# Three delays in the planner of a fused attention and state-space kernel: cold filler matmuls, TensorE results and ScalarE results

## The chip, the cores and the metric

The kernel runs on one core of a Trainium2 chip. The metric is the device time of one execution in microseconds (us); lower is better. Twelve runs of the kernel before the change gave a median of 744.47 us, between 743.07 and 746.74. One of them was recorded by the hardware profiler.

## The reference

Two independent blocks read two inputs of shape (1, 2048, 640), and their outputs are put side by side to (1, 2048, 1280), all in bf16.

```python
# A: state-space block (S5)
dt = exp(log_dt); Lam_bar = exp(dt * Lam); B_bar = ((Lam_bar - 1) / Lam)[:, None] * Bmat
Bu = einsum("bld,pd->blp", x, B_bar)
h_t = Lam_bar * h_(t-1) + Bu_t                     # over 2048 steps, 640 complex states
y = 2 * real(einsum("blp,dp->bld", h, Cmat)) + x * Dskip
# B: attention with 32 query heads of 20 columns and one shared key/value head
q = x @ wq; k = x @ wk; v = x @ wv
p = softmax(q k^T * 20 ** -0.5)                    # 32 heads x 2048 x 2048
o = (p v) @ wo
out = concatenate([y, o], axis=-1)
```

The softmax is most of the work: 32 x 2048 x 2048 exponentials. The kernel cuts them into 2048 tiles of 128 keys x 512 queries.

## The kernel before, in words

**The tiles.** For every tile a score matmul (`score`, recorded at L637 as `SC<-QT,KT`) writes 128x512 scores into a bank of PSUM. Most tiles are exponentiated on ScalarE: one `ACTIVATE` at L1218 takes two or three neighbouring banks at once (128x1024 or 128x1536) and writes bf16 into the tiles `PR`. The others, 495 of the 2048, are exponentiated on VectorE and GpSimd: the scores are scaled so that a rounding to an int16 is the bit pattern of the exponential, the first evacuation on VectorE (L652 `BIG<-SC` or `BIG<-MB`, 683 ns) makes one shifted copy, and three more copies with added constants (L652 `BIG<-BIG` on VectorE, L647 `BIG<-BIG,step` on GpSimd) make a better approximation as a weighted sum of four. The weights sit in the value tiles `VS`. A value matmul (L637 `MB<-PR,VP` or `MB<-BIG,VS`) then multiplies each exponentiated tile into one shared output bank, in groups of up to four that run side by side in four column groups of the array.

**The slots.** Six PSUM banks form two slots of three (`SC0`, `SC1`). ScalarE works on one while TensorE refills the other. A refill is one step of the plan, called a fill (`Build.fill`). In 456 of the fills the third bank of the slot is given to a VectorE tile ("own" tile), and ScalarE then takes two banks. The next fill of that slot waits for both readers, the `ACTIVATE` and the evacuation. Two more banks (`MB`) serve everything else: the projections, the state-space block, VectorE tiles outside the slots and the output bank.

**The order.** Nothing in the order of instructions is written by hand. Python code plays a schedule forward in time (`Schedule.run`): each step has an engine, a duration in ns and the steps that it depends on, and an engine that is free picks the ready step of best priority (`Schedule.pick`). The order so found is then emitted, engine by engine, with semaphore waits between engines (`Emitter`). So the delays in the schedule are not executed by the chip; they decide only which instruction stands before which in the five in-order queues. The chip waits for the semaphores, however long that takes. 24 schedules are made with small random shifts of the background work, and the one with the earliest planned end is emitted (`planned`).

**Delays.** When a step is seen by another engine, its planned end and a delay by the engine that produced it are added up:

```python
def seen(self, op, eng):
    if op.dma_key is not None:
        return op.end + self.OUT["dma"]
    if op.eng == eng:
        return op.end + self.OWN[eng] if eng in self.OWN else op.end
    return op.end + self.OUT[op.eng]
```

`OUT` is this table. `begin` also registers the moments at which the schedule looks again (`lag`), which have to contain the delays.

**Fillers.** At the start TensorE has little to do, and `warm_source` offers it matmuls of zeros (`MB<-PR`, 128x512) at the lowest priority, whenever the plan has it idle. Later, `keep_source` offers small groups of zeros (`MB<-KT,VZ`, 256 columns) when too little was issued in the last 3 us of the plan.

**The start and the end.** The first `ACTIVATE` of the softmax needs the transposed input, the keys and the first queries, whose weights come by DMA (`BIG<-in_B_wq_dram`). After the last one come the last value matmuls, the evacuation of the output bank (`pvsb`, L1585 and L1587), the division by the row sums, the last output projection (`WO`, `BT`) and five stores.

Of the kernel before, what the change touches and what calls it, by code (L numbers as in the profile page):

```python
# [42 lines left out]
class Schedule:  # L43
# [3 lines left out]


    ENGINES = ("pe", "act", "dve", "pool", "sp")
    OUT = {"pe": 200.0, "act": 130.0, "dve": 110.0, "pool": 150.0, "dma": 60.0}  # L50
    OWN = {"pe": 0.0, "act": 60.0, "dve": 115.0, "pool": 100.0}
    URGENT = 1.0

# [51 lines left out]
# [8 lines that stand above are left out]
    def done(self, ops):  # L113
        return all(o.end is not None and o.end + self.OUT.get(o.eng, 60.0) <= self.t for o in ops)

# [12 lines left out]
    def begin(self, op, eng):  # L128
        if op.hook is not None:
            op.hook(op)  # L130
        op.start = self.t
        if op.late:
            self.late_from = self.t + op.dur + self.PAUSE
        if eng == "pe":
            if op.mode != self.mode:
                op.dur += self.SWITCH
                self.mode = op.mode
            self.loads.append((self.t, op.load))
        if op.port:
            if eng == "pool" and self.port_last["dve"] is not None:  # L140
                op.after.append(self.port_last["dve"])
            self.port_free[eng] = self.t + op.dur + (self.LOCK if eng == "pool" else 0.0)
            self.port_last[eng] = op
            self.at(self.port_free[eng])
        if op.dma_key is not None:
            self.free[eng] = self.t + op.tail * len(op.fns)
            s = max(self.t + 1300.0, self.dma_free.get(eng, 0.0), self.pipe)
            self.dma_free[eng] = self.pipe = s + op.dur
            op.end = max(s + op.dur + 700.0, self.free[eng] + 1700.0) + op.land
        else:  # L150
            if op.table is not None and op.table != self.table:
                self.table = op.table
                op.dur += self.TABLE
            op.end = self.t + op.dur + op.tail
            self.free[eng] = self.t + op.dur - (self.EARLIER.get(eng, 0.0) if op.psum else 0.0)
        self.order.append(op)
        self.at(self.free[eng])
        for lag in (0.0, 60.0, 100.0, 110.0, 115.0, 130.0, 150.0, 200.0):
            self.at(op.end + lag)

    stay = staticmethod(lambda: True)
# [253 lines left out]
class Build:  # L415
# [284 lines left out]
    def warm_source(self):  # L700

        if self.pv_first or self.s.t > 40000.0:
            return None
        p = self
        if self.started:
            if self.s.recent(3000.0) > self.WARM:
                return None
            fns = self.four(self.pvbank, [p.VZ[:]] * 4, p.KT[:, 0:512], True, True)
            return Op("pe", fns, self.mmt(512), prio=3.5, mode="C", load=512.0, reads=["VZ", "KT0"], writes=[self.pvbank.key],
                      deps=[self.c_op["VZ"], self.kt_op[0]])  # L710
        return Op("pe", [self.mm(self.pvbank.ap, p.PR[:, 0, 0:128], p.PR[:, 0, :], True, True)], 260.0, prio=9,
                  load=512.0, deps=[self.zero_op], reads=["PR0"], writes=[self.pvbank.key], hook=self.warm_last)

    WARM = 4500.0
    V_AT, BOUND_AT = (-88, -87), -99

# [467 lines left out]
    def fill(self, op, i):  # L1184
# [21 lines left out]
        if first:  # L1206
            other = self.slot_last[1 - i][0]
            begin = self.s.t + self.mmt(512, 4) + 200
            if other.eng == "act":
                begin = max(begin, other.start + other.dur if other.start is not None else self.s.t + other.dur)  # L1210
            first[0].due = begin + 2 * (0.8333 * 1024 + 64) - self.REFILL
# [478 lines left out]
    def o_task(self, qb, k, bank, early=False):  # L1690
# [28 lines left out]
        for i in range(begin, upto):  # L1719
            if last:  # L1720
                yield lambda: all(n in self.norm_op for n in steps[i][0])
            prev = part(i, prev, i == begin)
# [581 lines left out]
```

## Time and profile before

The profiled execution took 743.07 us, and its span, from the first to the last instruction, is 741.2 us; 1.9 us lie around it. It was the fastest of the twelve runs, 1.4 us below their median.

| | before |
|---|---|
| median of 12 runs | 744.47 us (743.07 to 746.74) |
| profiled execution | 743.07 us, span 741.2 us |
| first `ACTIVATE` of the softmax begins | 22.1 us |
| last one ends | 732.2 us |
| softmax `ACTIVATE` instructions | 676: 475 of 1024 columns, 201 of 1536 |
| busy share: TensorE, VectorE, ScalarE, GpSimd | 96%, 90%, 97%, 57% |
| granted TensorE clock, mean of the span | 1.000 |

"Busy" of TensorE counts every matmul from its start to its modelled end, and matmuls overlap; 96% is not 96% of what it can do. "PEld" is the load of the stationary operand, and it is the instruction that waits when a matmul's data are late. Rows of a group give its number, its busy time and the mean of one, then the idle time ahead of its instructions and the engine that ended it. Rows of the timeline give start and length, both in us, then engine, line and operation.

### The profile page before, as it was taken

The page shows a single profiled execution, that of the slowest core. Times are in us where ns is not written, and L with a number is a line of the kernel's source. Part 1 is how long each engine was busy: PE and PEld are TensorE (multiplying, and loading weights), DVE is VectorE, ACT ScalarE, POOL GpSimd, SP SyncE. Part 2 cuts the span into 40 slices and gives each one's busy share as a digit, 9 for nine tenths or more (in the row PEclk, how much of TensorE's full clock was granted, in tenths as well). Part 3 has the DMA queues.
Part 4 walks back from the last instruction along what each step waited for, and adds up shares of the span by engine and source line. Part 5 has one row for each costly group of instructions (what it writes and reads, how often), then busy time and mean ns, then how long its engine had stood idle before and what let it go on. Part 6 is the DMA issues. An engine that isn't in the chain of part 4 may idle for free.

```text
span 741.2 us, 26646 instructions
## 1 busy us (share of the span) xinstructions
PE 708.2 (96%) x11322; PEld 256.5 (35%) x11323; DVE 664.6 (90%) x1367; ACT 722.6 (97%) x702; POOL 425.8 (57%) x448
## 2 busy tenths in 40 slices
PE   9999899998999999999999999989999999999997
PEld 3322222234443533333333333323333333332333
DVE  7888999989788798998899999998998998988995
ACT  5999999999999999999999999999999999999995
POOL 3866566420266558367476674567654845778460
PEclk9999999999999999999999999999999999999999
DMA  9414444364220100101100010110000010100001
GB/s 196 81 35 130 92 116 84 94 141 76 48 52 18 25 20 21 51 11 34 43 25 24 15 32 19 39 47 19 18 15 19 10 33 23 37 16 17 26 15 37
DMA packets 78089, 34.43 MB, mean 46 GB/s; under 512 B 58852, under 2 KB 77972, under 8 KB 77972
## 3 DMA queue, kind: packets, MB, share of 16 engines
q1 hardware_dynamic: 76352, 32.34, 18.4%
q8 instruction: 90, 1.47, 0.8%
q10 hardware_dynamic: 1620, 0.39, 0.3%
q14 instruction: 27, 0.22, 0.1%
HBM read 11.53 MB, written 9.75 MB: 29 GB/s over the span
## 4 chain that ended last, share of the span: by engine, by line
ACT 61%; PE 32%; DVE 5%; DMA 1%; issue 1%; ACTq 0%; DVEq 0%
ACT PR L1218 60%; PE MB L633 11%; PE SC L637 11%; PE MB L637 10%; DVE BIG L652 1%; DMA BIG<-in_B_wq_dram 1%; DVE prod L647 1%; DVE W L652 1%; DVE CT L647 1%; DVE CA L647 1%; PE SC L633 0%; DVE CT L651 0%; DVE CA L651 0%; DVE g L2046 0%; DVE pvsb L1580 0%
## 5 line engine op out<-in xcount | busy, mean ns | idle before, releaser
L1218 ACT ACTIVATE PR<-SC 128x1024 bf16<-128x1024 f32 (+1 forms) x676 | 708.4, 1260 | 2.3 <-PE SC L637 1.1
L647 POOL TENSOR_TENSOR BIG<-BIG,step 128x512 int32<-128x512 int32 x401 | 407.0, 1043 | 285.3 <-DVE BIG L652 162.6
L652 DVE TENSOR_SCALAR BIG<-SC 128x512 int16<-128x512 f32 x456 | 302.5, 683 | 38.8 <-PE SC L637 35.4
L637 PE MATMUL SC<-QT,KT 32*128 32x512 bf16 x2009 | 264.5, 384 | 24.1 <-ACT PR L1218 16.8
L637 PE MATMUL MB<-BIG,VS 128*32 128x512 bf16 x1980 | 247.0, 384 | 1.2 <-issue 0.6
L637 PE MATMUL MB<-PR,VP 128*32 128x512 bf16 x1553 | 216.0, 385 | 0.8 <-DVE pvsb L1580 0.6
L637 PEld LDWEIGHTS SC<-QT,KT 32*128 32x128 bf16 x2009 | 68.1, 91 | 258.5 <-ACT PR L1218 167.5
L652 DVE TENSOR_SCALAR BIG<-BIG 128x1024 int16<-128x1024 int16 (+1 forms) x356 | 128.8, 418 | 7.7 <-PE MB L637 6.4
L637 PEld LDWEIGHTS MB<-BIG,VS 128*32 128x32 bf16 x1980 | 62.8, 95 | 65.4 <-issue 43.0
L637 PEld LDWEIGHTS MB<-PR,VP 128*32 128x32 bf16 x1553 | 53.6, 94 | 54.1 <-issue 40.9
L633 PE MATMUL MB<-CT,W 128*32 128x320 bf16 (+2 forms) x1040 | 49.8, 301 | 0.2 <-DVE BIG L2006 0.2
L633 PE MATMUL MB<-xaT,BT 128*32 128x256 bf16 x800 | 34.5, 274 | 0.0
L633 PE MATMUL MB<-xaT,BA 128*32 128x256 bf16 x800 | 33.6, 274 | 0.1
L633 PE MATMUL MB<-CA,W 128*32 128x512 bf16 (+1 forms) x640 | 31.2, 302 | 0.0
L647 DVE TENSOR_TENSOR prod<-MB,tab 128x1024 bf16<-128x1024 f32 x20 | 24.3, 1215 | 3.8 <-PE MB L633 3.8
L652 DVE TENSOR_SCALAR BIG<-MB 128x512 int16<-128x512 f32 x39 | 26.5, 680 | 1.1 <-PE MB L637 0.7
L633 PEld LDWEIGHTS MB<-CT,W 128*32 128x32 bf16 x1040 | 21.5, 96 | 16.9 <-issue 7.9
L633 PE MATMUL MB<-WO,OP 128*32 128x128 bf16 (+1 forms) x576 | 26.5, 297 | 0.1
L1761 DVE CAST stg<-MB 128x512 bf16<-128x512 f32 x35 | 23.9, 682 | 2.6 <-PE MB L633 2.4
L633 PE MATMUL MB<-BIG 128*32 128x512 bf16 x340 | 25.6, 383 | 0.0
L2046 DVE TENSOR_TENSOR_SCAN g<-sc,hst,prod 128x256 bf16<-128x256 f32 x30 | 23.1, 774 | 0.0
L633 PEld LDWEIGHTS MB<-xaT,BA 128*32 128x32 bf16 x800 | 19.1, 96 | 9.0 <-issue 5.4
(167 smaller groups left out, 419.8 us busy)
## 6 DMA issues: line engine op xcount, KB each, us to landing
out_dram<-stg SPq DMA_DIRECT2D x31, 128.0 KB, 1.8
qd<-BIG SPq DMA_DIRECT2D x20, 128.0 KB, 1.8
QT<-qd SPq DMA_DIRECT2D x28, 80.0 KB
OP<-pvsb SPq DMA_DIRECT2D x105, 20.0 KB
rdP<-recs SPq DMA_DIRECT2D x105, 20.0 KB
W<-in_A_B_re_dram SPq DMA_DIRECT2D x10, 160.0 KB, 2.8
W<-in_A_B_im_dram SPq DMA_DIRECT2D x10, 160.0 KB, 2.8
lbd<-W SPq DMA_DIRECT2D x10, 160.0 KB, 1.9
```

Of the source, the lines that this page charges most:

```text
L633: r = e.matmul(out[32 * j:32 * j + 32], lhsT=lhsT[:, 32 * j:32 * j + 32], rhs=rhs, start=start, stop=stop, tile_position=(0, 32 * j), skip ...
L637: return lambda e: e.matmul(out, lhsT=lhsT, rhs=rhs, start=start, stop=stop, **kw)
L647: return lambda e: e.tensor_tensor(out, a, b, op)
L652: return lambda e: e.tensor_scalar(out, a, s1, s2, op0=op0, op1=op1)
L1218: ex = self.act(lambda e: e.activation(dst, t[:, 0:512 * n], ACT.Exp, scale=1.0 / UNIT), 0.8333 * 512 * n + 64, table="exp", deps=[op], re ...
L1761: ev = self.dve(lambda e: e.tensor_copy(st, bank.ap), 645, deps=[prev], reads=[bank.key], writes=[key], prio=self.EV, gate=(lambda: last.e ...
L2046: o = self.dve(lambda e, ri=ri, init=init: e.tensor_tensor_scan(p.g[:, u, ri, :], rdec, p.prod[:, 1, 0, ri, :], init, ALU.mult, ALU.add), ...
```

## The change

Three edits, all in the planner. The delay after which another engine sees a TensorE result in the plan goes from 200 to 215 ns, that of a ScalarE result from 130 to 225 ns; the list of moments at which the schedule looks again follows. A filler matmul at the start is planned at 450 ns until 6.0 us of planned time and at 240 ns after that, in place of 260 ns throughout.

```diff
-    OUT = {"pe": 200.0, "act": 130.0, "dve": 110.0, "pool": 150.0, "dma": 60.0}
+    OUT = {"pe": 215.0, "act": 225.0, "dve": 110.0, "pool": 150.0, "dma": 60.0}
...
-        for lag in (0.0, 60.0, 100.0, 110.0, 115.0, 130.0, 150.0, 200.0):
+        for lag in (0.0, 60.0, 100.0, 110.0, 115.0, 150.0, 215.0, 225.0):
...
-        return Op("pe", [self.mm(self.pvbank.ap, p.PR[:, 0, 0:128], p.PR[:, 0, :], True, True)], 260.0, prio=9,
+        return Op("pe", [self.mm(self.pvbank.ap, p.PR[:, 0, 0:128], p.PR[:, 0, :], True, True)], self.COLD if self.s.t < self.WARMED else 240.0, prio=9,
                   load=512.0, deps=[self.zero_op], reads=["PR0"], writes=[self.pvbank.key], hook=self.warm_last)
 
+    COLD, WARMED = 450.0, 6000.0
     WARM = 4500.0
```

No instruction is computed differently. What differs is the emitted order, and with it which tiles go to which engine. The counts of the two emitted programs:

| instructions | before | after |
|---|---|---|
| softmax `ACTIVATE`, 1024 columns | 475 | 463 |
| softmax `ACTIVATE`, 1536 columns | 201 | 210 |
| tiles exponentiated by ScalarE / by VectorE and GpSimd | 1553 / 495 | 1556 / 492 |
| first evacuations on VectorE from a slot (`BIG<-SC`) / from `MB` | 456 / 39 | 443 / 49 |
| copies of two tiles on VectorE / of one tile | 327 / 29 | 344 / 30 |
| copies of two tiles on GpSimd | 401 | 379 |
| fillers at the start (`MB<-PR`, 512 columns) | 23 | 16 |
| small zero matmuls (`MB<-KT,VZ`, 256 columns) | 356 | 292 |
| all instructions on TensorE (matmuls) | 11320 | 11244 |

The number of DMA issues is the same. The last `ACTIVATE` of the softmax has 1024 columns before and 1536 after.

## The prediction

> **What bounds the kernel now.** I read the page's busy shares first, then the costliest groups with shapes kept apart, then the waits, and last the timeline at the start, at one stall and at the end.
>
> ```profile
> PE 708.2 (96%) x11322; PEld 256.5 (35%) x11323; DVE 664.6 (90%) x1367; ACT 722.6 (97%) x702; POOL 425.8 (57%) x448
> ACT  5999999999999999999999999999999999999995
> ```
>
> ScalarE is full in 38 of 40 slices, so its length is the span.
>
> ```profile
> L1218 ACT ACTIVATE PR<-SC 128x1024 bf16<-128x1024 f32 x475 | 448.3, 1118 | 1.5 <-PE SC L637 1.0
> L1218 ACT ACTIVATE PR<-SC 128x1536 bf16<-128x1536 f32 x201 | 278.1, 1597 | 0.8 <-PE MB L637 0.4 <-PE SC L637 0.2
> ```
>
> Only 2.3 us of idle time are named in front of these, but a mean of 1118 ns hides stalls, because a record that waits or drains is long. Reading the 676 records one by one, from start to start, no 1024 is under 903 ns and no 1536 under 1330. The softmax runs from 22.14 to 732.17 us, 710.0 us. 474 intervals at 903, 201 at 1330 and the last record (about 1.2) make 696.5. **13.5 us are stall**, nearly all behind 1024s: 61 stalls over 50 ns hold 11.0 us, the rest are crumbs. With 22.1 ahead and 9.0 behind, these are all that the order can win without moving tiles off ScalarE.
>
> ```profile
> PEld SC L637 <- ACT PR L1218: 167.5, 414, 1.2
> POOL BIG L647 <- DVE BIG L652: 162.6, 41, 38.3
> PEld SC L637 <- DVE BIG L652: 60.7, 145, 0.9
> ```
>
> A fill stands at the head of TensorE's queue and waits 167.5 us in all for ScalarE to free the slot: the plan puts it there too early, and work that could run meanwhile stands behind it. One stall:
>
> ```profile
> 474.57 10.70 ACT L1218 ACTIVATE PR<-SC 128x1024 bf16<-128x1024 f32 x11
> ...
> 477.74 0.39 PE L637 MATMUL SC<-QT,KT 32*128 32x512 bf16 x3
> 478.06 0.39 PE L637 MATMUL MB<-BIG,VS 128*32 128x512 bf16 x2
> 478.34 0.83 PE L633 MATMUL MB<-CT,W 128*32 128x512 bf16 x12
> 479.10 0.39 PE L637 MATMUL SC<-QT,KT 32*128 32x512 bf16 x3
> ```
>
> The fill at 479.10 is issued behind 14 other matmuls; ScalarE starts on it 0.44 us later, at 479.54, 1300 ns after its last start where 903 would do. Sorting the 61 by what the fill last waited for: 12 (2.4 us) begin within 90 ns of the end of the slot's VectorE evacuation, 49 (8.6 us) stand behind other matmuls in TensorE's queue.
>
> **The change part by part.** The new delays run nowhere; they reorder. The delays of the trace: fill to `ACTIVATE` is 437 to 444 ns, which less the 219 ns that the plan gives a fill is 218 to 225, so 215 is right. From the planned end of an `ACTIVATE` (917 ns after its start) to the next fill of its slot it is never under 150 ns, and half of them are over 360, queues included. 130 was below anything seen; 225 lies above the floor.
>
> *Tiles.* ScalarE gets 12 fewer 1024s and 9 more 1536s: 9 x 1.330 - 12 x 0.903 = **+1.1 us**, on the path, with no cover; certain to some tenths.
>
> *Stalls behind TensorE's queue (8.6 us).* Between two fills the plan now leaves up to 95 ns more for other groups before the fill. I priced the emitted orders with trace rows (216 ns for a group of 512 columns, from nine fillers in 2.12 us with a last drain of 0.38; about 95 for a change between score and other groups, the fill issues 308 after such a group): gaps between fills whose TensorE work exceeds ScalarE's interval by over 100 ns are 139 before, 124 after; over 200 ns, 65 and 56. If stalls fall with that count, 11% of 8.6 is 0.9 us. If each of the 49 shrinks by the 95 ns by which the plan was short, it is 4.7. A smaller gain would need the new order to be worse where it counts better. The long stalls, such as the 397 ns above, come from three or more groups in a row, which 95 ns does not break; I take **-2.5**, between.
>
> *Stalls behind VectorE (2.4 us).* VectorE gets 17 more two-tile copies (429 ns each), one more single (286) and 3 fewer first evacuations (683): +5.5 us on an engine with 76.6 us idle, since GpSimd makes 22 fewer. GpSimd itself, 57% busy, is on no path. Against it, 13 fewer fills (443 for 456) have an evacuation of their own to wait for. The bound below is -0.5 (a fifth of these stalls gone); above, +3, if over half of the 5.5 lands in front of evacuations that a fill waits for. I take **+0.4**, nearer to the small end, because 60.7 us of such waits on TensorE cost ScalarE only 2.4 now.
>
> *Fillers.* In the trace a filler costs 427 ns cold and 216 warm, and the granted clock is full from 4.6 us on.
>
> ```profile
> 1.24 2.32 PE L637 MATMUL MB<-PR 128*128 128x512 bf16 x5 [1.24 <-DVE sel L755]
> ...
> 6.25 2.12 PE L637 MATMUL MB<-PR 128*128 128x512 bf16 x9
> 8.21 1.06 PE L637 MATMUL SC<-ident,CT 128*128 128x128 bf16 x16
> 9.42 0.39 PE L637 MATMUL MB<-BIG 128*20 128x512 bf16 x4 [0.16 <-DMA BIG<-in_B_wq_dram]
> ```
>
> The plan thought that 20 fillers of 260 would be through before the transposes of 8.21; they were late. Now 12 stand there, and the transposes can start up to 1.0 us earlier. But the next group waits for the query weights, which land at 9.29 whatever TensorE does, and from 9.42 to 18.26 TensorE never waits, with the same work after as before. So the first softmax `ACTIVATE` stays at 22.1: **0**, from -0.3 (transposed tiles ready earlier) to +0.3 (five more small value matmuls ahead of the first fill).
>
> What speaks against it is the clock. By the rows, after 4.6 us fillers cost 216, yet the plan charges 450 until its 6.0 us, which is 6.9 of the profile, as its zero is VectorE's first memset at 0.91. So TensorE will idle about 0.2 us per filler there, and some 0.7 ahead of the transposes and 1 ahead of the weights. [...] Bounding it from rows alone: if the 8.8 us of work from 9.42 ran cold for 3.4 us (the time from the first matmul at 1.24 to 4.63), it would lose 1.7 us. I keep that as a small risk.
>
> *The end.* Before, the last `ACTIVATE` has 1024 columns and only one or two value groups remain after it:
>
> ```profile
> 732.02 0.59 PE L637 MATMUL MB<-BIG,VS 128*32 128x512 bf16 x5
> 732.24 0.38 PE L637 MATMUL MB<-PR,VP 128*32 128x512 bf16 x2
> 732.45 0.82 PE L633 MATMUL SC<-WO,OP 128*32 128x512 bf16 x12
> ...
> 736.47 0.61 PE L633 MATMUL SC<-BT,pvsb 128*32 128x512 bf16 x8
> ```
>
> `pvsb` starts at 732.68, 0.5 us after ScalarE's last record ends. After, five groups of output projection and then 13 value matmuls (four groups, the first with the last tiles) follow that end in the queue: 24 value matmuls and 20 projections after the last fill (about 2.4 us) end some 0.2 us behind it, then 4 x 0.213 and a drain of 0.39, so `pvsb` starts 1.2 us after it: +0.7. Three projection groups that ran after the division (736.04 and around) now run before: -0.64 on TensorE, but the last of three VectorE outputs ends only 0.25 before ScalarE's store, so -0.25. Together **+0.5**, from 0 to +0.9.
>
> 64 small zero matmuls less (16 groups of 110 ns) are free: TensorE waits 167.5 us anyway. DMA issues on SP keep their number; their waits are not on the chain.
>
> Sum: 1.1 - 2.5 + 0.4 + 0 + 0.5 = **-0.5 us**: 742.6 against the profiled 743.07, and 744.0 against the median of 744.47, which lies 1.4 above it. About 0.2% (1.5 us) is what a measurement of this kernel can tell from no change.
>
> **The rivals.**
>
> *Order wins (faster).* ScalarE's stalls behind TensorE's queue shrink by the whole 4.7 and VectorE costs nothing: 1.1 - 4.7 + 0.5 = -3.1, 741.4. For: the 167.5 us of waits at fills, and that 130 lies below the least delay of the trace. Against: the long stalls come from bunched groups, and 124 of 139 stay.
>
> *VectorE holds the fills (slower).* The copies that GpSimd gave up stand in VectorE's queue ahead of evacuations of slots; each late evacuation holds the fill at L637 and all of TensorE behind it, and ScalarE stalls. Price: +3 in place of +0.4, with only 0.9 won behind TensorE: 1.1 - 0.9 + 3 + 0.5 = +3.7, 748.2. It decides once stalls behind VectorE exceed about 5 us (2.4 now). For: 90% busy and 5.5 us more. Against: 13 fewer such fills.
>
> *It does nothing (no change).* The chip waits by semaphore and not by plan; the change only draws another order of like quality: 1.1 + 0.5 = +1.6 with the stalls unchanged, 746.1, the upper edge of no change.
>
> **How the numbers follow.** The forecast (stalls down by 1 to 3.5, the sum within 1.5 of zero) gets 0.38; order wins, 0.31; VectorE holds, 0.20; no gain at all, 0.11, of which half falls in no change. So faster 0.32, same 0.40, slower 0.28, some of the forecast's edges going to either side. The range for 8 in 10 goes down to -3.6 (4.7 and a VectorE gain of 0.5) and up to +3.5, short of the slow rival's centre: 740.9 to 748.0.
>
> **What would show it.** Right: the softmax begins at 22.1 +-0.3; its records sum to 697.5 without stalls, and stalls are 11 to 12 us; waits of `PEld SC L637` for ScalarE fall below 167.5; `pvsb` starts over 1 us after the last softmax record. Wrong: stalls above 13.5 or below 9; over 5 us of them begin within 90 ns of an evacuation; a granted clock below full after 5 us; a first `ACTIVATE` beyond 22.6.

## The result, and the profile after

The changed kernel takes **751.49 us** (median of 8 runs, 749.67 to 753.39; a ninth, at 749.84, is on record with its clock), 0.9% more than before: ratio 1.0090, 95% interval 1.0074 to 1.0105. That is 7.5 us above the forecast and 3.5 above the upper end of the range. The profiled execution took 751.28 us with a span of 749.5, against 741.2 before.

The page first: busy shares, ScalarE's slices and the granted clock's slices.

```profile
PE 713.8 (95%) x11246; PEld 255.3 (34%) x11247; DVE 662.5 (88%) x1382; ACT 725.7 (97%) x699; POOL 401.6 (54%) x426
ACT  5799999999999999999999999999999999999995
PEclk9799999999999999999999999999999999999999
```

ScalarE's share is still 97%, but its second slice (18.7 to 37.5 us) has dropped from 9 to 7, and so has the clock there. Before, every slice of the clock was a 9. The shares say nothing of this: VectorE and TensorE are even a little less busy.

The groups of the softmax `ACTIVATE`, shapes kept apart (count, then busy time and mean in ns, then idle time before them):

```profile
L1219 ACT ACTIVATE PR<-SC 128x1024 bf16<-128x1024 f32 x463 | 439.3, 1101 | 6.7 <-PE SC L637 4.5 <-PE MB L637 1.4
L1219 ACT ACTIVATE PR<-SC 128x1536 bf16<-128x1536 f32 x210 | 290.8, 1633 | 0.5 <-PE SC L637 0.5
```

The counts are those of the emitted program. Idle time ahead of the 1024s has grown from 1.5 to 6.7 us. Read from start to start, with 903 and 1330 ns taken off as before, the span splits so:

| us | before | after | difference |
|---|---|---|---|
| first softmax `ACTIVATE` begins | 22.12 | 22.38 | +0.26 |
| records without stalls, last record included | 696.55 | 697.68 | +1.13 |
| stalls while the clock is full | 13.50 | 14.69 | +1.19 |
| stalls while the clock is at half | 0 | 5.06 | +5.06 |
| after the last softmax record | 9.06 | 9.74 | +0.68 |

The differences add up to 8.3, which is that of the two spans. Some 60% of it arises while TensorE runs at half clock: in the profiled run from 28.94 us for 10.24 us, and from 424.89 for 3.41. The windows around the first of them show it. Each row has the window, its length, then busy time (and instructions) of PE, PEld, VectorE, ScalarE and GpSimd, then the granted clock; the last two numbers are the share of the DMA engines and GB/s. Before:

```profile
25.53:28.94 3.41, 3.10 (x36) 1.13 (x28) 2.83 (x8) 3.41 (x5) 3.07 (x7) 1.00 0.44 98
28.94:32.36 3.42, 3.36 (x53) 1.37 (x51) 2.30 (x7) 3.42 (x5) 2.91 (x7) 1.00 0.19 43
32.36:35.77 3.41, 3.41 (x46) 0.97 (x46) 2.70 (x6) 3.41 (x4) 2.00 (x3) 1.00 0.11 38
35.77:39.18 3.41, 3.41 (x48) 0.86 (x40) 3.09 (x6) 3.41 (x5) 3.18 (x4) 1.00 0.13 43
```

After:

```profile
25.53:28.94 3.41, 2.95 (x41) 1.69 (x38) 3.31 (x15) 3.41 (x5) 3.03 (x7) 1.00 0.39 88
28.94:32.36 3.42, 3.42 (x32) 0.94 (x28) 1.49 (x4) 2.81 (x3) 2.94 (x8) 0.50 0.18 40
32.36:35.77 3.41, 3.41 (x24) 0.48 (x21) 1.68 (x3) 2.05 (x2) 0.69 (x2) 0.50 0.10 33
35.77:39.18 3.41, 3.41 (x28) 0.65 (x25) 1.98 (x3) 2.05 (x2) 2.04 (x2) 0.50 0.10 34
```

In the three windows at half clock TensorE is busy without a break and issues 84 matmuls (32, 24, 28) in place of 147 (53, 46, 48). ScalarE works 2.05 of 3.41 us in two of them and waits for fills. For these 10 us TensorE is the bound and not ScalarE. What came just before is in the timeline of TensorE (start, length, engine, line, operation, number). Before:

```profile
23.88 0.39 PE L637 MATMUL SC<-BIG 128*20 128x512 bf16 x4
24.20 0.39 PE L637 MATMUL SC<-QT,KT 32*128 32x512 bf16 x2
24.52 0.61 PE L637 MATMUL SC<-BIG 128*20 128x512 bf16 x8
25.06 0.39 PE L637 MATMUL SC<-QT,KT 32*128 32x512 bf16 x2
25.38 0.61 PE L637 MATMUL SC<-BIG 128*20 128x512 bf16 x8
...
27.18 0.40 PE L637 MATMUL MB<-PR,VP 128*32 128x512 bf16 x4
```

After:

```profile
22.57 1.04 PE L637 MATMUL SC<-BIG 128*20 128x512 bf16 x16
23.54 0.39 PE L637 MATMUL SC<-QT,KT 32*128 32x512 bf16 x2
23.86 0.39 PE L637 MATMUL SC<-BIG 128*20 128x512 bf16 x4
...
25.29 0.39 PE L637 MATMUL SC<-QT,KT 32*128 32x512 bf16 x2 [0.28 <-ACT PR L1219]
25.51 0.28 PE L986 MATMUL MB<-mab,pick 20*128 20x1 f32 x2
25.72 0.29 PE L936 MATMUL SC<-wvr,BIG 128*128 128x20 bf16 x5
...
27.12 0.39 PE L637 MATMUL SC<-QT,KT 32*128 32x512 bf16 x2 [0.31 <-ACT PR L1219]
27.35 0.28 PE L986 MATMUL MB<-mab,pick 20*128 20x1 f32 x2
...
28.36 0.61 PE L637 MATMUL MB<-PR,VP 128*32 128x512 bf16 x8
```

Between the fills stand matmuls of 1 and of 20 columns. They fill the "busy" column, because the profile gives each of them 0.16 to 0.27 us up to its modelled end, however few its columns. A better measure is to count each matmul by its columns at 0.417 ns, side-by-side ones once; then one of 20 columns counts for 8 ns. (The third group of 512 columns in a row follows the second at 427 ns at half clock, in after at 31.21 us, and at 216 at full clock, in before at 31.08; the count takes half of the 427, 0.417 a column.) This estimate gives the share of a window in which columns stream: **42%** in 25.53 to 28.94, and **39%** in 421.47 to 424.89, the two windows after which the clock falls. No gap between streams in them is longer than 0.6 us. In before, the same stretch from 25.53 to 28.94 has 60%; the thinnest windows of its profiled run have 45% and 48%, and the clock stays full. Before, the second query projection (`SC<-BIG`, 20 matmuls with 512 columns) was spread from 23.88 to 25.99 between fills, and the first value matmul came at 27.18. After, 16 of the 20 stand in one block from 22.57 to 23.6 ahead of the third fill, and the first value matmul comes at 28.36; from 24.4 to 28.4 only the fills themselves and one other group (at 26.09) are wide.

The waits (total, number, longest):

```profile
PEld SC L637 <- ACT PR L1219: 163.4, 400, 0.9
POOL BIG L647 <- DVE BIG L652: 161.5, 52, 22.8
...
PEld SC L637 <- DVE BIG L652: 56.9, 131, 0.9
```

Both waits of the fills have gone down, from 167.5 and 60.7, and yet the stalls have gone up, from 13.5 to 19.8 us. One reading is that the fills that wait less came later to the head of TensorE's queue.

The end is as predicted. The last softmax record ends at 739.80, and `pvsb` starts 1.16 us later:

```profile
738.18 1.62 ACT L1219 ACTIVATE PR<-SC 128x1536 bf16<-128x1536 f32 x1
...
740.96 0.38 ACT L1586 ACTIVATE pvsb<-MB 128x256 bf16<-128x256 f32 x1 [1.16 <-PE MB L637]
```

**All runs, not one.** Each run has a mean granted clock, and (1 - clock) x 2 x span is the time that it spent at half clock, as the clock records of the traces of before and after hold 1.0 and 0.5 alone (13.5 us by this for the profiled run of after, 13.65 in its trace). In 110 runs of before the median is 4.5 us, in 9 of after 13.5. Fitted over the runs, each us at half clock costs 0.28 us before and 0.39 after; at full clock the fits give 743.3 and 746.5. So of the 7 us between the medians about 3.8 belong to half clock (13.5 x 0.39 - 4.5 x 0.28 = 4.0; the slope of after, from nine runs, is uncertain by 0.07, which makes about 1 us here) and about 3.2 would remain at full clock. In the profiled runs that is tiles 1.1, stalls 1.2, end 0.7, start 0.26. No run of after was at full clock, so its 746.5 is an extrapolation.

### The profile page after: what moved, and what is told of

Its sections match the earlier page's. It is cut to its first block, busy times and chain, and to the rows that moved or that the text cites. A ratio compares the mean times of both kernels' runs of the same rounds, so it can differ in the third digit from the quotient of the medians.

```text
span 749.5 us, 26447 instructions
## 1 busy us (share of the span) xinstructions
PE 713.8 (95%) x11246; PEld 255.3 (34%) x11247; DVE 662.5 (88%) x1382; ACT 725.7 (97%) x699; POOL 401.6 (54%) x426
## 3 DMA queue, kind: packets, MB, share of 16 engines
q1 hardware_dynamic: 76352, 32.34, 18.7%
## 4 chain that ended last, share of the span: by engine, by line
ACT 63%; PE 31%; DVE 2%; SPq 1%; DMA 1%; issue 0%; DVEq 0%
ACT PR L1219 63%; PE SC L637 10%; PE MB L637 10%; PE MB L633 10%; DVE BIG L652 1%; PE SC L633 1%; SPq L622 1%; DMA BIG<-in_B_x_dram 1%; DVE prod L647 1%; PE SC L936 0%; SPq L618 0%; DVE PR L647 0%; DVE pvsb L1581 0%; DVEq L470 0%; DVE pvsb L1588 0%
## 5 line engine op out<-in xcount | busy, mean ns | idle before, releaser
L647 POOL TENSOR_TENSOR BIG<-BIG,step 128x512 int32<-128x512 int32 x379 | 382.8, 1039 | 316.2 <-DVE BIG L652 161.5
L652 DVE TENSOR_SCALAR BIG<-SC 128x512 int16<-128x512 f32 x443 | 294.2, 683 | 38.4 <-PE SC L637 35.9
L637 PE MATMUL SC<-QT,KT 32*128 32x512 bf16 x1999 | 265.5, 387 | 24.5 <-ACT PR L1219 17.7
L637 PE MATMUL MB<-PR,VP 128*32 128x512 bf16 x1556 | 218.3, 387 | 0.4 <-DVE pvsb L1581 0.4
L637 PEld LDWEIGHTS SC<-QT,KT 32*128 32x128 bf16 x1999 | 68.0, 91 | 261.0 <-ACT PR L1219 163.4
L652 DVE TENSOR_SCALAR BIG<-BIG 128x1024 int16<-128x1024 int16 (+1 forms) x374 | 135.4, 419 | 6.1 <-PE MB L637 4.3
L637 PEld LDWEIGHTS MB<-BIG,VS 128*32 128x32 bf16 x1968 | 60.4, 95 | 68.6 <-issue 45.7
L652 DVE TENSOR_SCALAR BIG<-MB 128x512 int16<-128x512 f32 x49 | 33.3, 680 | 4.7 <-PE MB L637 4.6
L633 PE MATMUL MB<-xaT,BT 128*32 128x256 bf16 x800 | 37.0, 275 | 0.0
L633 PE MATMUL MB<-WO,OP 128*32 128x128 bf16 (+1 forms) x576 | 27.5, 297 | 0.0
L633 PEld LDWEIGHTS MB<-CT,W 128*32 128x32 bf16 x1040 | 20.6, 96 | 17.8 <-issue 9.5
L1581 DVE CAST pvsb<-MB 128x512 bf16<-128x512 f32 x31 | 21.2, 682 | 5.5 <-PE MB L637 5.1
L633 PEld LDWEIGHTS MB<-xaT,BT 128*32 128x32 bf16 x800 | 19.4, 96 | 11.1 <-issue 8.8
```

What stands on the lines that cost most here:

```text
L633: r = e.matmul(out[32 * j:32 * j + 32], lhsT=lhsT[:, 32 * j:32 * j + 32], rhs=rhs, start=start, stop=stop, tile_position=(0, 32 * j), skip ...
L637: return lambda e: e.matmul(out, lhsT=lhsT, rhs=rhs, start=start, stop=stop, **kw)
L647: return lambda e: e.tensor_tensor(out, a, b, op)
L652: return lambda e: e.tensor_scalar(out, a, s1, s2, op0=op0, op1=op1)
L1581: ev = self.dve(lambda e: e.tensor_copy(p.pvsb[:, slot, :], bank.ap), 645, deps=[op], reads=[bank.key], writes=[f"pvsb{slot}", f"pvsb{slot ...
```

## The experiments

Three theories. A: the order has thin windows, the clock falls after them, and the stalls of those stretches are the loss. B: the longer delays themselves make a worse order at full clock. C: the fillers bring the clock up late, and all else follows from that. Against all stood the rival that the change only drew an unlucky order. The table has all runs; "falls" are those of the profiled run before the end of the softmax, and stalls are split by whether the clock was full or at half. The ratio is estimated from all runs and need not be the quotient of the two medians.

| kernel | median us | ratio to before, 95% interval | us at half clock, median | falls at, us | stalls at full / at half clock, us |
|---|---|---|---|---|---|
| after | 751.49 | 1.0090 (1.0074 to 1.0105) | 13.5 | 28.9, 424.9 | 14.7 / 5.1 |
| e_fill | 747.30 | 1.0026 (1.0003 to 1.0048) | 10.4 | none | 14.4 / 0 |
| e_delays | 748.59 | 1.0078 (1.0040 to 1.0115) | 10.5 | 99.1, 594.1 | 14.9 / 2.9 |
| e_early | 751.45 | 1.0087 (1.0060 to 1.0113) | 17.2 | 27.6, 505.5 | 13.7 / 5.8 |
| e_dense | 750.33 | 1.0085 (1.0056 to 1.0114) | 6.7 | 421.8 | 17.7 / 0.5 |
| e_dense2 | 750.67 | 1.0062 (1.0037 to 1.0088) | 11.2 | 28.8, 424.8, 506.7 | 14.7 / 4.9 |
| e_seed23 | 749.77 | 1.0068 (1.0048 to 1.0088) | 10.5 | 27.5, 423.4 | 14.7 / 3.1 |
| e_before5 | 744.85 | 1.0011 (0.9987 to 1.0036) | 0.7 | none | 14.3 / 0 |
| e_act150 | 750.54 | 1.0073 (1.0050 to 1.0097) | 12.0 | none | 12.6 / 0 |
| e_lateq | 747.68 | 1.0038 (1.0023 to 1.0052) | 6.7 | none | 17.8 / 0 |
| e_akeep | 748.43 | 1.0054 (1.0035 to 1.0073) | 14.9 | 27.2, 593.8 | 13.2 / 3.3 |
| e_bkeep | 747.82 | 1.0054 (1.0033 to 1.0075) | 6.0 | 25.4, 510.1 | 13.2 / 7.0 |
| e_bdense | 744.73 | 0.9997 (0.9987 to 1.0008) | 3.0 | 500.7 | 14.0 / 1.1 |
| e_fillq | 750.77 | 1.0083 (1.0059 to 1.0106) | 17.2 | 26.6, 504.5 | 14.4 / 5.8 |
| e_bq | 743.17 | 0.9981 (0.9962 to 1.0000) | 0.7 | 716.0 | 14.1 / 1.5 |
| e_act180q | 748.12 | 1.0042 (1.0026 to 1.0057) | 10.4 | 26.6 | 15.0 / 2.0 |
| e_150q | 745.95 | 1.0020 (0.9999 to 1.0041) | 0 | none | 13.4 / 0 |
| e_bthin | 747.95 | 1.0047 (1.0031 to 1.0062) | 23.1 | 167.3, 501.8 | 13.3 / 1.6 |
| e_bwide | 745.96 | 1.0022 (1.0011 to 1.0034) | 4.5 | 501.2 | 14.6 / 1.8 |

The kernel before had a median between 744.34 and 744.66 beside these runs.

### One part of the change at a time

The delays alone (e_delays), and the filler edit alone (e_fill):

```diff
 e_delays
-    OUT = {"pe": 200.0, "act": 130.0, "dve": 110.0, "pool": 150.0, "dma": 60.0}
+    OUT = {"pe": 215.0, "act": 225.0, "dve": 110.0, "pool": 150.0, "dma": 60.0}
 e_fill
-        ... 260.0, prio=9,
+        ... self.COLD if self.s.t < self.WARMED else 240.0, prio=9,
```

> The two delays alone (215 and 225 ns), the filler planned at 260 ns as before. The query projection stands spread between the fills here, as in before. Theory A: no fall at 29 us, so the clock term is gone; what is left is the tiles (1 fewer 1024 than before, so -0.9 us), the end (last instruction of 1536 columns, up to +0.7) and the other stalls: 743 to 747. Theory D (the delays make the slower order): 748 or more without any fall.

> The filler's edit alone (450 ns until 6.0 us, then 240), delays 200 and 130. The query projection stands bunched in front of the third fill as in after, but the first value matmul comes two fills earlier. Theory A: a fall near 29 us if the window there holds under about 43% of matmul time: 747 to 750; without a fall, 744 to 746 (the tiles are those of before). Theory D: as before, 744.6.

Each alone is slower than before, by 4.1 and 2.8 us. The filler edit is the clearer one. Its ten runs fall into two heaps: three at full clock (743.83 to 744.08) and seven with a mean clock of 0.988 to 0.995 (746.33 to 749.37). The 11 runs of before at full clock have a median of 743.5, so at full clock little is lost, and nearly the whole loss is half clock. The tiles are those of before (475 and 201). The thinnest windows of its profiled run, at 22.7 and 500.5 us, have 46% and 44%, near those of before, and the clock held there; where it fell in the other runs no profile shows. The delays cost both ways: 14.9 us of stalls at full clock and 2.9 at half, and the first softmax record at 23.62 us, since the rise came at 6.97 there (4.63 in before) and the transposes behind the 20 fillers began 1.0 us later. Neither expectation of e_delays was met: no fall near 29 us, but two later ones, and a time above 748 that is not free of falls.

### Is it the late rise of the clock (theory C)?

Eight fillers of the changed kernel doubled, which closes the idle time that the 450 ns make:

```diff
+                pe = [op for op in plan.s.order if op.eng == "pe"]
+                end = next(i for i, op in enumerate(pe) if "xn0" in op.reads)
+                for op in [op for op in pe[:end] if "PR0" in op.reads and len(op.fns) == 1][-8:]:
+                    op.fns = op.fns * 2
```

> The order of after, with eight fillers of the start issued twice, so that 20 stand ahead of the first transposes as before. Theory A (thin work at 25.5 to 28.9 us): the clock rises near 4.6 us, but still falls near 29 us if the thin stretch lies in one window; 750 to 752, or less if the windows lie otherwise. Theory C (the late rise at 8.5 us, from the thin start, is what leads to the fall): rise at 4.6 us, no fall, 747 to 748.

The clock rose at 7.13 us in place of 8.46 and still fell at 27.61, for as long as without the edit; the time is the same. The rise came 1.3 us earlier, not the 3.9 us that the test was meant to give; what settles theory C are the other profiles. e_150q rose at 9.46 us and never fell, e_bkeep rose at 4.93 and fell at 25.4. A late rise is neither needed for a fall nor enough for one. (The rise is not a property of the order alone: before, e_bdense, e_bwide and e_bthin have the same order up to the first fill and rose at 4.63, 5.72, 6.23 and 6.87 us.)

### Is it the thin stretch of the start (theory A)?

Groups of zeros, as `warm_source` uses them, put ahead of the small matmuls in the stretch: eight (e_dense), three (e_dense2), and three in the kernel before (e_bdense).

```diff
+                zero = plan.four(plan.pvbank, [plan.VZ[:]] * 4, plan.KT[:, 0:512], True, True)
+                for op in pe[begin:end]:
+                    if "pick" in op.reads or "wvr" in op.reads:
+                        op.fns = zero + op.fns
```

> The order of after, with eight groups of zero matmuls (four of 512 columns each, as the fillers of the start) put in front of the small matmuls (L986, L936) between the first fill and the first value matmul. Theory A (the granted clock falls at 28.9 us because the 3.4 us before it hold too little TensorE work, and the 10.2 us at half clock cost ScalarE 4.2 us of its 6.3 us of new stalls): full clock from the start to 400 us, 4 us less than after, so 747 to 748; up to 1 us of that is taken back by the extra groups. Theory B (the order itself is worse, the clock is a by-product): the stalls between 29 and 40 us stay, 751 to 752.

> The order of after with only three of the eight zero groups, in front of the first, fourth and fifth of the small matmuls at L986, where TensorE waits for ScalarE anyway. Theory A: no fall near 29 us, and without the 2.4 us of stalls that the eight groups cost around 26 us, so 4 us under after: 747 to 748 where no window falls later, 748 to 749 where one does. Theory B: 751.

> The order of before, with three zero groups of 4 x 512 columns put in front of small matmuls at L985 between the first fill and the first value matmul, where TensorE waits. If the start of before sometimes falls too (its window from 21.7 us holds 48% matmul time), half-clock time goes from 4.5 us per run to 1 to 2, and the median from 744.4 to 743.3 to 743.8: a version better than both. If before falls elsewhere, no change: 744.4.

With eight groups the fall at 29 us is gone and half-clock time is halved, but the groups stand ahead of fills and cost some 2.4 us of stalls themselves; the time improves by 1 us only, short of the 747 to 748 expected. Three groups were not enough in the profiled run, which still fell at 28.84, although its window then had 56%: the one fall in this case after a window above 50%. Its median, 750.67, is near the 751 of theory B, but as the fall stayed it decides nothing. Of its ten runs, the two at full clock took 746.26 and 747.53, which is what the fit of after says for full clock. In the kernel before the three groups leave the median where it was (0.9997). None of its 12 runs is over 745.65, where 4 of the 22 runs of before beside it are and the highest is 746.68; that is a hint of a safer start and no more.

The next test gives TensorE no extra work and only spreads what is there. The second query projection waits for the first four tiles, which puts it between the fills as in the kernel before:

```diff
-        T.append((-98.5, 0, self.first_made, lambda bank: self.qt_task(bank, 1)))
+        T.append((4, 0, self.first_made, lambda bank: self.qt_task(bank, 1)))
```

> All of after, but the second query projection may begin only after four tiles, so that its groups stand between the second and fifth fills, spread as in before, and the first value matmul comes earlier. 465 instructions of 1024 columns and 207 of 1536: -1.1 us of ScalarE against before. Theory A (the bunched projection empties the stretch at 25 to 29 us and the clock falls there): no fall at 27 to 29 us in the profile, cold time per run down from 13.5 us by about 8, and 746 to 748. Theory G (falls come wherever windows lie, the start is no worse than other places): cold time about as in after, 749 to 751.

Two of its windows in the stretch where the clock of after fell:

```profile
25.53:28.94 3.41, 3.15 (x43) 1.07 (x35) 3.10 (x13) 3.41 (x5) 3.08 (x7) 1.00 0.41 89
28.94:32.36 3.42, 3.42 (x54) 1.30 (x52) 2.14 (x6) 3.42 (x5) 2.97 (x8) 1.00 0.16 34
```

The first has 63% where after has 42%. There is no fall in the whole profile, ScalarE is full in the windows from 25.53 to 39.18 (3.41 of 3.41 us), and the stalls between 22 and 40 us go from 4.3 us in after to 0.2. That supports A for the start. The median is 3.8 us lower (747.68), but this is a sum of several things: its tiles cost 2.1 us less than those of after, and its stalls at full clock, 17.8 us, are 3.1 more, nearly all of it after 40 us. So the time by itself does not say what the fall had cost.

### The same order, only thinner

Each experiment so far adds groups to the order or changes it. The last pair does neither: the kernel before in its own emitted order, instruction by instruction, with only its 356 small zero matmuls made 16 columns wide (e_bthin) or 512 (e_bwide) in place of 256.

```diff
-        fns = [... bank.off:bank.off + 256], p.VZ[:], p.KT[:, 0:256], ...
+        fns = [... bank.off:bank.off + 16], p.VZ[:], p.KT[:, 0:16], ...
```

> The kernel before in its own emitted order; only the 356 small zero matmuls are 16 columns wide in place of 256. The tiles sum stays 695.4. With the trace of before and those matmuls at 16 columns, 5 windows of 3.413 us would be under 42% filled with matmuls, and none is as it stands. Theory (a thin window makes the clock fall): about 5 falls, 15 to 35 us at half clock, each costing 0.28 to 0.44: a median of 748 to 753, with stalls in the half-clock stretches. Rival (falls and stalls both come from a poor order; zero matmuls only stand in the way): the time of before or up to 1 us less, 743.5 to 745, with no more half clock than before.

> The kernel before in its own emitted order; the 356 small zero matmuls are 512 columns wide in place of 256, 89 groups of 107 ns more. Theory: windows in the middle fuller, half clock only from the start or none, stalls up by what the longer groups hold up (at most 89 x 0.107 = 9.5 us if each stood ahead of a late fill, more likely 0.5 to 2): a median of 744 to 746. Rival (zero matmuls only stand in the way): as much slower as the thin kernel is faster.

The thin kernel is 3.6 us slower with *less* work on TensorE, and its runs spend 23.1 us at half clock against 4.5; the rival is out. Its time lies at the lower edge of what was expected (747.95 for 748 to 753). Its profiled run, the fastest of six, fell twice where five falls were expected, after a window with 32% and one with 41%. Rows of the first, in e_bthin:

```profile
163.88:167.30 3.42, 2.00 (x46) 0.77 (x37) 3.28 (x7) 3.42 (x4) 0.00 (x0) 1.00 0.32 65
167.30:170.70 3.40, 2.95 (x45) 0.87 (x46) 3.16 (x8) 3.40 (x4) 0.00 (x0) 0.50 0.58 100
```

and of before at the same place, where that window has 54%:

```profile
163.88:167.30 3.42, 2.62 (x53) 1.16 (x53) 3.25 (x7) 3.42 (x4) 0.00 (x0) 1.00 0.50 96
167.30:170.70 3.40, 2.62 (x50) 0.98 (x42) 3.16 (x8) 3.40 (x4) 0.00 (x0) 1.00 0.50 106
```

(The 0.32 and 0.50 in the last columns but one are the DMA share, not this count.) So with the order unchanged, thinner windows alone bring the falls in this kernel. Here ScalarE stays full in the row at half clock (3.40 of 3.40), because TensorE has slack in that stage (2.95 of 3.40 busy at half clock); what a fall costs depends on the stage in which it comes (0.5 us of stalls over 10.2 us here, 5.1 over 13.7 in after). The zero matmuls have a price too: e_bwide at full clock takes 745.5 (three runs), 2.2 more than the 743.3 of before. For e_bthin a line through its six runs reaches 741.0 at full clock, but none of them is above 0.991, and its profiled run has 13.3 us of stalls at full clock against 13.5, so that a gain there is not shown. The wide kernel is within its 744 to 746, but it spends no less time at half clock than before (4.5 us): its profiled run fell after a window with 40% at 498 us. The zero matmuls are not free, as the prediction had priced them; at 256 columns they are worth it here, with 744.34 us against 747.95 at 16.

### Luck of the draw?

One seed in place of the best of 24 schedules, of the changed kernel (e_seed23) and of the kernel before (e_before5); and `KEEP`, the threshold of the small zero matmuls, from 3500 to 4500 in both (e_akeep, e_bkeep).

```diff
-        for seed in range(self.PLANS):
+        for seed in (23,):
```

> All of after, with another of its 24 draws of the background work (the planner's start order is the same in all draws). It has 465 instructions of 1024 columns and 209 of 1536, +1.1 us against before as after has. Theory E (the loss is the luck of one draw): 745 to 748, or as far off on the other side. Theory A (the loss comes from the start order and from delays, which all draws share): 749 to 753 with a fall near 29 us.

> Before, with another of its 24 draws. 478 instructions of 1024 columns and 199 of 1536, +0.05 us against before. Theory E: anywhere in 742 to 750. Theory A: the start order is that of before, no fall near 29 us: 743 to 747.

> After, with the threshold of the small zero groups raised from 3500 to 4500 columns in 3 us (652 of these matmuls for 292). The start order is that of after. Theory A: the fall at 27 to 29 us stays (these groups begin only with the first value matmuls), the later ones near 424 us go: 3 us of half clock less, 749 to 751. Theory G: no falls at all, 746.

> Before, with the same threshold (780 of the small matmuls for 356). 469 instructions of 1024 columns and 208 of 1536, +3.9 us of ScalarE against before. Half-clock time per run from 4.5 us to near 0 if falls come in the thin places inside the softmax: 746 to 748 in all, by the tiles. If the clock is no matter, the same 746 to 748 but with spread as in before (743 to 750 there).

One other draw on each side keeps its side: 749.77 with the edits, 744.85 without; and the draw of the changed kernel falls at nearly the same two places. So it is not a single unlucky order. With more zero matmuls the changed kernel takes 748.43, 3.1 us less, but not by the clock, as theory A had it: its runs spend 14.9 us at half clock, no less than the 13.5 of after, and the later fall moved to 593.8 us. What is lower in its profile are the tiles (by 0.9 us) and the stalls (13.2 and 3.3 us). The kernel before gets slower (747.82): its tiles on ScalarE cost 3.5 us more (last record left out), its half-clock time did not go to near 0 but to 6.0 us, and its profiled run fell at the start too, after a window with 47%. Two of the ten runs of e_before5 fell to a mean clock of 0.988 and 0.989 and took 751.07 and 749.16. The kernel before does not own a safe start: its window from 21.7 us has 48%, and that of e_bkeep, after which the clock fell at 25.4, has 47%.

### How much of it is the delay (theory B)?

ScalarE's delay at 150, the least seen in the trace (e_act150); then the late projection with the delays of before (e_fillq), with 180 (e_act180q) and 150 ns (e_150q), and the late projection alone, without any edit of the change (e_bq).

> After, with ScalarE's delay at 150 ns, the least that the trace of before shows between the planned end of an instruction and the next fill of its slot, in place of 225. It has 461 instructions of 1024 columns and 214 of 1536: +4.6 us of ScalarE against before. Here the first value matmul stands one fill earlier than in after. Theory F (225 is too long: the plan puts fills late and ScalarE waits): stalls outside cold stretches fall below the 13.5 us of before, towards 10; time 746 to 749 because of the tiles. Theory A: depends on the clock alone; 747 to 749 without a fall, 751 and more with one near 29 us.

> The filler edit with the second query projection put behind the first four tiles, delays as before (200 and 130 ns). Theory (the longer delay makes real stalls at full clock): stalls 13.5 to 15 us against 17.8 with the new delays in the same start order; no fall of the clock before 40 us; tiles sum 697.2, so a span of 742.5 to 744.5 and a median of 744 to 746. Rival (the spread start costs the stalls, not the delay): stalls 17 to 18 us here too and a median of 747 to 749.

> The change with 180 ns in place of 225 ns for ScalarE results, and the late second projection. Tiles sum 695.9. Theory: stalls between those of the old and the new delay, 14.5 to 16.5 us, median 744.5 to 747. Rival (stalls do not go by the delay): 17 to 18 us, as with 225, or any other order; median 747 to 749.

> The change with 150 ns, the least delay seen in the trace of before, for ScalarE results, and the late second projection. Tiles sum 698.9. Theory: stalls 12.5 to 14.5 us as with 150 and the early projection (12.6), median 745.5 to 747.5, the loss being tiles. Rival: stalls 17 us or more, median above 749.

> The kernel before with the second query projection behind the first four tiles; no edit of the change. ScalarE's softmax records sum to 693.7 us without stalls, 1.7 less than before. Theory: stalls 13.5 to 15 us, no fall at the start, median 742 to 744, a little faster than before. Rival: the spread start costs stalls, 17 us or more, median 746 to 748.

Stalls at full clock, one row for each delay (left out are e_early, e_dense and e_dense2, which repeat the order of after with matmuls added, and e_bdense, e_bthin and e_bwide, which repeat that of before):

| delay of ScalarE results | orders | stalls at full clock, us |
|---|---|---|
| 130 | before, e_before5, e_fill, e_bkeep, e_fillq, e_bq | 13.5, 14.3, 14.4, 13.2, 14.4, 14.1; mean 14.0 |
| 150 | e_act150, e_150q | 12.6, 13.4 |
| 180 | e_act180q | 15.0 |
| 225 | after, e_delays, e_seed23, e_akeep, e_lateq | 14.7, 14.9, 14.7, 13.2, 17.8; mean 15.1 |

The two orders with 150 are among the four lowest, and no order with 225 is below 13.2. But the step from 130 to 225 is 1.1 us of mean with 13.2 to 17.8 inside one row, so the dose is a tendency and not shown. e_fillq missed its expected time (750.77 for 744 to 746): with the old delays, too, the late projection left a window at 23.2 us with 42%, and the clock fell at 26.6. Spreading the projection is no cure by itself; it depends on what the rest of the order puts there. e_act180q missed in time for the same reason, with a fall at 26.6 us (its four runs with a mean clock of 0.997 took 745.86 to 746.39, the others 747.1 to 750.0). e_150q met its numbers: 7 of 12 runs at full clock at 745.3 to 746.0, the loss being its tiles (698.0 us of records against 695.4, last record left out). e_act150 had the fewest stalls of all, though not the 10 us expected, but its runs spend 12 us at half clock and its tiles cost 4.2 us more.

e_bq is the one version below both, at 743.17 us: 0.9981 (0.9962 to 1.0000), the edge of what can be told from no change. Its plan gave ScalarE 481 and 195 records, 6 x 1.330 - 6 x 0.903 = 2.6 us less than before (the 1.7 of the expectation counts the last record on one side alone), and eight of twelve runs have a mean clock of 0.999 or 1.000. The lower sum of the tiles can account for its gain; no run separates it from the spread.

## Why the prediction was wrong, point by point

*Start*: 22.38 for 22.1 +-0.3: right, though with some luck, as the first softmax record lies anywhere from 22.1 to 23.6 us in the profiled runs of this case. *Tiles*: +1.1 for +1.1: right. *End*: +0.7 for +0.5, with `pvsb` 1.16 us after the last record: right, within the bounds.

*The clock* is the step that failed most. The prediction asked in "Fillers" whether the clock would come up in time, priced a cold stretch behind 9.42 us at 1.7 us, and added 0. It priced no fall later in the run. No run of the changed kernel shows that 0, as none was at full clock: in its place the profiled run has 5.1 us of stalls at half clock, and the fits over all runs give about 4. The thin stretch could have been read before: the order showed the projection moved ahead of the third fill, and the profile of before had two windows with 45% and 48%, the least of its run, one of them (from 21.7 to 25.1 us) at the edge of that stretch. In the runs here all falls lie on multiples of 3.413 us from the rise, and they go with how full the whole window is, not with its longest gap: the windows ahead of 23 of the 24 falls were 32 to 50% full and that of the other one 56%, and the longest gap in any of them was 1.05 us, while a window of before with a gap of 1.11 us (from 390.3 us, 57% full) kept the clock.

*Stalls behind TensorE's queue* is the second failed step: -2.5, bounded by -4.7 and -0.9. Sorted as in the prediction, stalls over 50 ns behind other matmuls went from 49 with 8.6 us to 79 with 16.4, of which about 5 at half clock: +2.8 at full clock. The count that was to stand for them, gaps with over 100 ns of surplus work, went from 139 to 124, so it does not measure them. The bound that left no room for a loss rested on that count. One reading is that the planner, told that a slot comes free 95 ns later, puts another group ahead of the fill, and that on the chip, where the trace of before has 150 ns at the least, this group is then in the way. It fits the tendency in the table of delays, but no run shows it alone, and why these stalls grew at full clock stays open.

*Stalls behind VectorE*: +0.4, with -0.5 as the lower bound. They fell from 2.4 to 1.0 us (12 stalls to 5): wrong in sign. It fits that the 13 fewer fills with an evacuation of their own weighed more than the 5.5 us of extra copies; no run separates the two. The slow rival "VectorE holds the fills" (748.2) therefore had the right side and the wrong mechanism.

*What would show it*: the two signs of "wrong" that name stalls above 13.5 and a granted clock below full after 5 us both appeared. The sign of "right", waits for ScalarE below 167.5, appeared too, at 163.4, and meant nothing.

## What to carry to other kernels

In this case the clock fell, before the end of the softmax, only after windows of 3.413 us in which columns streamed for 32 to 56% of the time. When a change reorders TensorE in a kernel like this one, cut the new order into windows of the length that the falls show and count the streaming columns in each; gaps and the profile's busy share did not tell (ahead of the first fall of after no gap was over 0.6 us, and TensorE counts as busy for 2.95 of 3.41 us). The kernel before, whose thinnest windows have 45% and 48%, gave 742.65 to 749.63 us over 32 runs, and this reorder cost it 0.9%; so read the mean clock of all runs before one profile is explained. And a planner's delay set above the least that the trace shows is not safer for that: the two orders planned with 150 ns stall for 12.6 and 13.4 us at full clock, the five with 225 ns for 13.2 to 17.8. This is a tendency of a few orders and not a rule.

## What the hardware showed that was not expected

Over the profiles of this case (20 kernels, windows at full clock before the end of the softmax, cut at 3.413 us from the rise), the share of a window in which columns stream goes with whether the clock falls at its end:

| share of the window | windows | followed by a fall |
|---|---|---|
| under 42% | 14 | 14 |
| 42 to 46% | 17 | 6 |
| 46 to 50% | 19 | 3 |
| 50 to 60% | 279 | 1 |
| over 60% | 3890 | 0 |

No sharp edge shows in this count, which takes nothing but columns; the one fall above 50% is that of e_dense2 at 28.84 us. After a fall the clock stayed at half for one to four windows: 3.41 us at the shortest, 10.24 for the first fall of after, 13.65 in e_bkeep. One us at half clock cost 0.28 to 0.44 us of time in most kernels by fits over their runs, and the price differs by stage: the two falls of after cost 5.1 us of stalls over 13.7, that at 167 us in e_bthin 0.5 over 10.2.
